# A graph tensor product on one core: second-pass chunks of 12 tiles, parts of 0.31, 0.36 and 0.33, and a loop over all edges behind a count of rows

## The chip, the cores and the metric

The kernel runs on one core of a Trainium2 chip. The metric is the time of one execution on the device, in microseconds (us). Three runs of the kernel before took 8667.58, 8670.53 and 8680.19 us; their median is 8670.53.

The core has five engines with instruction streams of their own: PE (matrix products), DVE (vector work), ACT (functions of one operand), POOL (here: the indirect DMAs, that is gathers and scatters by a list of row numbers) and SP (the other DMAs). They wait for each other through semaphores.

## The reference

There are 10000 nodes with 64 channels of 4 components (x), and 640000 edges, each with a source node, a destination node, four numbers Y and four numbers edge_feat. Sources and destinations are drawn at random.

```
R   = silu(edge_feat @ w_rad)                      # (E, 64)
xs  = x[src]                                       # (E, 64, 4)
tp  = einsum('eci,ef,ifo->eco', xs, Y, cg)         # (E, 64, 4)
msg = R[:, :, None] * tp
agg = segment_sum(msg.reshape(-1, 256), dst, N).reshape(N, 64, 4)
out = einsum('ncm,cd->ndm', agg, w_mix)
```

## The kernel before

**Sorting.** To sum without conflicts, the kernel first sorts the edges by destination in two passes. An edge travels as 9 words (a key that holds destination and source, Y, edge_feat). The edges lie as 5000 tiles of 128. The first pass puts them into 18 groups of 576 destinations, the second puts a group into its 18 buckets of 32 destinations; there are 313 buckets. Both work on chunks of T tiles: T is 12 in the first pass and 11 in the second (L109). In a chunk, the edges of one group (bucket) are packed into rows of r edges: r is 14 in the first pass, 15 in the second. PE does the packing: for each tile of the chunk a one-hot matrix of 128 x 128 (L588 on DVE, L594 and L595 on ACT for six of the tiles, act in L48) times X, the edge's words spread over the r slots of a row (L569, L572). The products of a chunk add up in one PSUM tile `pr` (L602), so a chunk may fill at most 128 rows. ACT copies it to `rt` (L609), and POOL scatters the rows to DRAM with one indirect DMA (L613, `store`).

**Carried rows.** In the second pass (carry) a bucket's last row of a chunk, when it isn't full, is not stored but carried: PE adds it in the next chunk with one more product (L604). `tables` (L351) works out for a whole segment which row every chunk's buckets begin at, from counts that PE makes (L365). In it `st` holds the first row of each bucket in a chunk, and `inc` the running number of rows, whose last column is the number of rows of the chunk.

**Parts.** The edges are cut into three parts by their position (SPLIT, L36): 0.3, 0.355 and 0.345 of the 5000 tiles, rounded to 24. A bucket has 17 tiles of 128 slots in DRAM, of which part 0 is given 5 and parts 1 and 2 six each. What doesn't fit into a part's tiles lies in the next part's; what doesn't fit into 145 rows of a bucket goes to an overflow list.

**Messages.** For each part, group and bucket the kernel works on a unit: POOL gathers 128 source rows of x for each of the unit's 5 or 6 tiles with an indirect DMA each (L893, into one of 7 `xg` buffers), DVE multiplies them by the radial function (L945) and builds S from Y and the destination within the bucket (L935, L938), and PE sums over the edges (L958) into `G`. After the last part the weights are applied (L1006) and the output is written (L1015). There are 939 units and 5321 gathers.

**Order.** The first pass of part 0 runs alone, together with the clearing of buckets and groups. From then on `groups` (L1039) writes the order of PE, DVE and ACT by hand: it walks the quarters of the units of part k and puts between them steps of the first pass of part k+1 and of the second pass of the next segment (a part's group), by their shares of steps (`pass2_steps`). The smallest group comes first in each part, and is sorted before the part's messages begin. In each engine's stream the order is fixed.

**The end.** `overflow` (L1118) takes up the overflow list of each pass: a count is loaded into the engines' registers (L1131), and a loop runs its body for each 128 slots of the list (L1136 to L1199); the body computes 128 messages and adds them to the output rows with an indirect read (L1166) and an indirect write (L1199). For the first pass's list it writes the pass's number of rows in the same way.

Of the kernel before, what the change touches and what calls it, by code (L numbers as in the profile page):

```python
# [18 lines left out]
F = mybir.dt.float32  # L19
BF = mybir.dt.bfloat16  # L20
I32 = mybir.dt.int32
OP = mybir.AluOpType
# [12 lines left out]
UT = 6  # L35
SPLIT = ((0.3, (5,)), (0.355, (6,)), (0.345, (6,)))  # L36
LG = 5
# [8 lines left out]
class Pass:  # L46


    def __init__(self, T, r, cap, act, carry):
        self.T, self.r, self.cap, self.act, self.carry = T, r, cap, act, carry  # L50
        self.stride = 1 << (cap + P - 1).bit_length()
        self.rw = r * W

        assert T * P + B * (2 * r - 2 if carry else r - 1) < (P + 1) * r and cap >= P

# [18 lines left out]
class Kernel:  # L74
    def __init__(self, ctx, tc, x, src, dst, Y, ef, w_rad, cg, w_mix, out):
# [32 lines left out]
        self.p1 = Pass(T, r, max(map(max, self.gt)) * P // r, 6, False)  # L108
        self.p2 = Pass(11, 15, BT * P // 15, 6, True)  # L109

# [14 lines left out]
        self.xw = max(q.T * q.rw for q in (self.p1, self.p2))  # L125
        assert max(q.T + q.carry for q in (self.p1, self.p2)) <= 12

# [16 lines left out]
    def consts(self):  # L144
# [74 lines left out]
        self.bc = c.tile([P, B], F, name="bc")  # L219
        nc.vector.memset(self.bc, float(self.p2.cap))  # L220

    def clear_groups(self, k, eng):
# [128 lines left out]
    def tables(self, ps, D, nt, rows, kov, base, cap):  # L351
# [6 lines left out]
        assert N <= ps.NC <= 26 and nt >= T  # L358
        NC = ps.NC
        w = lambda nm, k, p=P, b=1, d=F: wk.tile([p, k], d, name=nm, tag=nm + ps.key, bufs=b)  # L360
# [12 lines left out]

        sums = w("sums", B * (T + 1))
        nc.vector.tensor_tensor_scan(sums[:H], ps.on, ps.cols, 0.0, op0=OP.mult, op1=OP.add)
# [37 lines left out]
        nc.vector.tensor_tensor(st[:H, :B], inc[:H], R[:H], op=OP.subtract)  # L413
        nc.vector.tensor_copy(st[:N, B:], inc[:N, B - 1:])

        first, at = w("first", B), w("at", T * B)
        if ps.carry:
# [17 lines left out]
        eye = self.ident[:N, :N].unsqueeze(2).to_broadcast([N, N, J])  # L435
        bs, bd = w("bs", NC * J, NC, d=BF), w("bd", NC * J, NC)
        blk = lambda t: t[:N, :N * J].rearrange("p (c j) -> p c j", j=J)
# [74 lines left out]
    def route(self, ps, quad, nt, table):  # L512
# [65 lines left out]
        def rows(c):  # L578
# [253 lines left out]
    def messages(self):  # L832
# [19 lines left out]
        def index(k):  # L852
# [265 lines left out]
    def overflow(self, ps, count):  # L1118
# [14 lines left out]

        def body(k):
            pay = wk.tile([P, W], F, name="opay")
            nc.sync.dma_start(pay, flat[bass.ds(k * (P * W) + ps.ovf * ps.rw, P * W)].rearrange("(s w) -> s w", w=W))  # L1136
# [7 lines left out]
            xg = wk.tile([P, 64, 4], F, name="oxg")  # L1144
            nc.gpsimd.indirect_dma_start(  # L1145
                out=xg.rearrange("p c i -> p (c i)"), out_offset=None, in_=self.x,
                in_offset=bass.IndirectOffsetOnAxis(ap=si, axis=0))

            pd = pm_.tile([P, 512], F, name="opd", tag="misc", bufs=1)
            nc.tensor.matmul(pd[:, :P], dst.to_broadcast([P, P]), self.ident, start=True, stop=True)  # L1150
            eq = wk.tile([P, P], F, name="oeq")
            nc.vector.tensor_scalar(eq, pd[:, :P], dst, None, op0=OP.is_equal)

            dup = wk.tile([P, P], F, name="odup")
            nc.vector.tensor_tensor(dup, eq, self.L, op=OP.mult)
            skip = wk.tile([P, 1], F, name="oskip")
            nc.vector.tensor_reduce(skip, dup, axis=AX.X, op=OP.max)
            em = wk.tile([P, 1], F, name="oem")
            nc.vector.tensor_scalar(em, dst, 0.5, None, op0=OP.is_lt)
            nc.vector.tensor_tensor(skip, skip, em, op=OP.max)  # L1160
            di = wk.tile([P, 1], I32, name="odi")
            nc.vector.scalar_tensor_tensor(skip, skip, FAR, dst, op0=OP.mult, op1=OP.add)
            nc.vector.tensor_scalar(di, skip, -1.0, None, op0=OP.add)
            cur = wk.tile([P, 256], F, name="ocur")
            nc.vector.memset(cur, 0.0)
            nc.gpsimd.indirect_dma_start(  # L1166
                out=cur, out_offset=None, in_=self.out, in_offset=bass.IndirectOffsetOnAxis(ap=di, axis=0),
                bounds_check=self.N - 1, oob_is_err=False)

            pT = pm_.tile([P, 512], F, name="opT", tag="misc", bufs=1)  # L1170
            nc.tensor.transpose(pT[:W, :P], pay, self.ident)
            sT = wk.tile([W, P], F, name="osT")
            nc.scalar.activation(sT, pT[:W, :P], AF.Copy)
            pr = pm_.tile([P, 512], F, name="opr", tag="misc", bufs=1)
            nc.tensor.matmul(pr[:, :80], sT, self.wo, start=True, stop=True)
            R = wk.tile([P, 64], F, name="oR")
            nc.scalar.activation(R, pr[:, :64], AF.Silu)
            A = wk.tile([P, 16], F, name="oA")
            nc.scalar.activation(A, pr[:, 64:80], AF.Copy)
            V = wk.tile([P, 64, 4], F, name="oV")  # L1180
            nc.vector.tensor_tensor(V, xg, R.unsqueeze(2).to_broadcast([P, 64, 4]), op=OP.mult)
            M = wk.tile([P, 64, 4], F, name="oM")
            for o in range(4):
                nc.vector.tensor_scalar(M[:, :, o], V[:, :, 0], A[:, o:o + 1], None, op0=OP.mult)
                for i in range(1, 4):
                    nc.vector.scalar_tensor_tensor(M[:, :, o], V[:, :, i], A[:, 4 * i + o:4 * i + o + 1],
                                                   M[:, :, o], op0=OP.mult, op1=OP.add)
            pm = pm_.tile([P, 2, P], F, name="opm", tag="misc", bufs=1)
            for h in range(2):
                nc.tensor.matmul(pm[:, h, :], M[:, 32 * h:32 * h + 32, :].rearrange("p c o -> p (c o)"), eq,  # L1190
                                 start=True, stop=True)
            ms = wk.tile([P, 2, P], F, name="oms")
            nc.scalar.activation(ms, pm, AF.Copy)
            po = pm_.tile([P, 512], F, name="opo", tag="misc", bufs=1)
            for h in range(2):
                nc.tensor.matmul(po[:, :256], ms[:, h, :], self.wx[:, h].rearrange("p d o -> p (d o)"),
                                 start=(h == 0), stop=(h == 1))
            nc.vector.tensor_tensor(cur, cur, po[:, :256], op=OP.add)
            nc.gpsimd.indirect_dma_start(  # L1199
                out=self.out, out_offset=bass.IndirectOffsetOnAxis(ap=di, axis=0), in_=cur, in_offset=None,  # L1200
                bounds_check=self.N - 1, oob_is_err=False)

        with tc.For_i(0, n, 1) as k:  # L1203
            body(k)

    def run(self):
# [63 lines left out]
```

## Time and profile before

| what | value |
|---|---|
| median of three runs | 8670.53 us (8667.58 to 8680.19) |
| span of the profiled execution | 8660.7 us |
| median of the runs less that span | 9.8 us |
| instructions | 149335 |
| mean granted TensorE clock | 0.894 |
| gathers (L893) | 5321 |
| first-pass chunks (stores to grp, L613) | 417 |
| second-pass chunks (stores to bkt, L613) | 541 |
| data moved by DMA | 1056.64 MB, mean 122 GB/s |

The profile shows one execution; its span reaches from the first to the last instruction, and no other time is given for that execution. In a row of a group stand the line of the code, the engine, the operation, the tile written and those read, the count, the busy time and the mean time in ns of one, and the idle time of the engine just before, with what ended most of it. "issue" there means that the engine waited for nothing that the profile shows. In a row of a stretch stand its bounds and length, then for PE, PEld (weight loads), DVE, ACT and POOL the busy time and the number of instructions, then the granted clock of PE (1.00 is full), the busy share of the DMA engines and GB/s. In a row of the waits stand the waiting instruction, what it waited for, and the total, the number and the longest of the waits. In a row of the timeline stand the start and length in us.

### The profile page before, as it was taken

The page shows a single profiled execution, that of the slowest core. Times are in us where ns is not written, and L with a number is a line of the kernel's source. Part 1 is how long each engine was busy: PE and PEld are TensorE (multiplying, and loading weights), DVE is VectorE, ACT ScalarE, POOL GpSimd, SP SyncE. Part 2 cuts the span into 40 slices and gives each one's busy share as a digit, 9 for nine tenths or more (in the row PEclk, how much of TensorE's full clock was granted, in tenths as well). Part 3 has the DMA queues.
Part 4 walks back from the last instruction along what each step waited for, and adds up shares of the span by engine and source line. Part 5 has one row for each costly group of instructions (what it writes and reads, how often), then busy time and mean ns, then how long its engine had stood idle before and what let it go on. Part 6 is the DMA issues. An engine that isn't in the chain of part 4 may idle for free. (4 is left out here: it accounts for less than half of the span.)

```text
span 8660.7 us, 149335 instructions
## 1 busy us (share of the span) xinstructions
PE 6942.9 (80%) x52148; PEld 6380.0 (74%) x52148; DVE 7173.7 (83%) x13741; ACT 4089.0 (47%) x11736; POOL 6041.3 (70%) x6308
## 2 busy tenths in 40 slices
PE   7978888888888778888888888866888878788875
PEld 6867777777777677777777777766777767777764
DVE  8989899889998788999989998877877768677754
ACT  6866555555556455454544554433333323333310
POOL 1236777667777767777777777777777777777775
PEclk9989999889999889999889899888998889888887
DMA  9313434334433434444444444444444444444442
GB/s 169 104 58 99 123 115 119 103 113 117 121 110 111 122 106 132 135 132 138 133 130 136 135 133 134 128 138 132 128 125 125 125 124 124 122 128 125 124 123 83
DMA packets 696289, 1056.64 MB, mean 122 GB/s; under 512 B 252018, under 2 KB 500226, under 8 KB 695536
## 3 DMA queue, kind: packets, MB, share of 16 engines
q0 software_dynamic: 286560, 746.71, 30.3%
q1 hardware_dynamic: 406384, 292.76, 12.2%
q8 instruction: 412, 6.75, 0.3%
q10 hardware_dynamic: 2592, 7.63, 0.3%
q14 instruction: 341, 2.79, 0.1%
HBM read 856.08 MB, written 207.12 MB: 123 GB/s over the span
## 5 line engine op out<-in xcount | busy, mean ns | idle before, releaser
L893 POOL DMA_INDIRECT xg<-in_x_dram,sidx x5321 | 5067.8, 952 | 1739.3 <-issue 1386.5
L602 PE MATMUL pr<-X,oh 128*128 128x126 f32 (+1 forms) x21112 | 2765.2, 289 | 395.7 <-ACT rt L609 215.6
L958 PE MATMUL G<-S,xg 128*128 128x128 f32 x21284 | 2953.1, 302 | 98.1 <-DVE Gp L987 62.8
L602 PEld LDWEIGHTS pr<-X,oh 128*128 128x128 f32 x21112 | 2638.2, 201 | 477.8 <-ACT rt L609 264.2
L958 PEld LDWEIGHTS G<-S,xg 128*128 128x128 f32 x21284 | 2803.5, 215 | 139.3 <-DVE Gp L987 86.2
L945 DVE TENSOR_TENSOR xg<-xg,pre 128x1536 f32<-128x1536 f32 (+1 forms) x939 | 1556.8, 1658 | 710.5 <-DMA xg<-in_x_dram,sidx 586.4
L594 ACT ACTIVATE sq<-i,rowf 128x128 f32<-128x128 f32 x5605 | 1735.7, 393 | 13.9 <-DVE rowf L559 13.4
L572 DVE TENSOR_TENSOR X<-dv,Wt 128x1512 f32<-128x1512 f32 (+4 forms) x958 | 1588.4, 1658 | 149.0 <-PE pr L602 94.8
L927 ACT ACTIVATE pre<-pre 128x384 f32<-128x384 f32 (+1 forms) x939 | 430.8, 459 | 1694.7 <-PE pre L924 1204.7
L595 ACT ACTIVATE oh<-sq,ones 128x768 f32<-128x768 f32 (+3 forms) x958 | 932.1, 973 | 32.9 <-issue 5.5
L938 DVE TENSOR_TENSOR S<-dv,pay 128x768 f32<-128x768 f32 (+1 forms) x939 | 857.4, 913 | 48.0 <-PE G L958 2.8
L613 POOL DMA_INDIRECT grp<-rt,idx x417 | 415.5, 996 | 585.9 <-ACT rt L609 240.1
L588 DVE TENSOR_TENSOR oh<-dv,rowf 128x640 f32<-128x640 f32 (+2 forms) x922 | 792.2, 864 | 0.5
L613 POOL DMA_INDIRECT bkt<-rt,idx x541 | 543.2, 1004 | 221.7 <-issue 125.8
L911 PE MATMUL pre<-identb,e 128*108 128x128 bf16 x1878 | 277.3, 231 | 523.4 <-DVE xg L945 513.6
L911 PEld LDWEIGHTS <-e 128*108 128x108 bf16 x1878 | 219.9, 133 | 604.5 <-issue 515.2
L916 ACT ACTIVATE sT<-pre 108x256 bf16<-108x256 f32 x939 | 353.5, 376 | 631.1 <-PE pre L911 628.4
L1006 PE MATMUL po<-wf,Gs 128*128 128x256 f32 (+2 forms) x1392 | 382.3, 436 | 150.7 <-DVE Gs L987 150.5
L542 ACT ACTIVATE pc<-pp 128x432 f32<-128x432 f32 (+3 forms) x506 | 243.7, 482 | 524.1 <-DVE pos L551 407.3
L1006 PEld LDWEIGHTS po<-wf,Gs 128*128 128x128 f32 (+2 forms) x1392 | 277.5, 205 | 238.3 <-DVE Gs L987 166.8
L609 ACT ACTIVATE rt<-pr 128x135 f32<-128x135 f32 (+1 forms) x958 | 258.8, 273 | 269.4 <-DMA bkt<-rt,idx 181.4
L923 PE MATMUL pre<-wr,sT 108*128 108x192 bf16 x939 | 240.2, 256 | 142.2 <-ACT sT L916 141.8
(240 smaller groups left out, 5309.3 us busy)
## 6 DMA issues: line engine op xcount, KB each, us to landing
xg<-in_x_dram,sidx POOLq DMA_INDIRECT x5321
sums<-Gp SPq DMA_DIRECT2D x626, 128.0 KB
old<-sums SPq DMA_DIRECT2D x626, 128.0 KB
bkt<-z SPq DMA_DIRECT2D x24, 994.5 KB
pay<-bkt SPq DMA_DIRECT2D x34, 486.0 KB
ys<-in_Y_dram SPq DMA_DIRECT2D x104, 96.0 KB
es<-in_edge_feat_dram SPq DMA_DIRECT2D x104, 96.0 KB
out_dram<-ot SPq DMA_DIRECT2D x69, 128.0 KB
```

Source lines behind the costliest of these rows:

```text
L572: nc.vector.tensor_tensor(X[:, :m, :].rearrange("p t (s w) -> p t s w", w=W), msk.unsqueeze(3).to_broadcast([P, m, ps.r, W]), QD[c // Q][1 ...
L588: nc.vector.tensor_tensor(oh[:, :v, :], self.v128.unsqueeze(1).to_broadcast([P, v, P]), row[:, o:o + v].unsqueeze(2).to_broadcast([P, v, P ...
L594: nc.scalar.activation(sq[:, u, :], self.i128, AF.Square, bias=to, scale=-1.0)
L595: nc.scalar.activation(oh[:, v:v + len(at), :], sq[:, :len(at), :], AF.Relu, bias=self.ones[:, 0:1], scale=-2.0)
L602: nc.tensor.matmul(pr[:, :ps.rw], oh[:, u, :], X[:, u, :], start=(u == 0), stop=(not on and u == m - 1))
L613: st = nc.gpsimd.indirect_dma_start(out=ps.dst, out_offset=bass.IndirectOffsetOnAxis(ap=idx[:, i:i + 1], axis=0), in_=RT.pop(c), in_offset ...
L893: nc.gpsimd.indirect_dma_start(out=xg[:, t, :], out_offset=None, in_=self.x, in_offset=bass.IndirectOffsetOnAxis(ap=si[:, u:u + 1], axis=0))
L911: nc.tensor.matmul(pre[:KR, 256 + 128 * h:384 + 128 * h], e[:, 36 * t:36 * t + KR], self.identb, start=True, stop=True)
L938: nc.vector.tensor_tensor(S[:, :ut], self.eq[:, :ut].unsqueeze(3).to_broadcast([P, ut, NB, 4]), pb[:, :, 1:5].unsqueeze(2).to_broadcast([P ...
L945: nc.vector.tensor_tensor(V, V, R.unsqueeze(3).to_broadcast([P, ut, 64, 4]), op=OP.mult)
L958: nc.tensor.matmul(G[:, h].rearrange("p n f -> p (n f)"), V[:, t, 32 * h:32 * h + 32, :].rearrange("p c i -> p (c i)"), S[:, t].rearrange( ...
L1006: nc.tensor.matmul(po[:nn, :256], Gs[:, h, f].rearrange("p b n -> p (b n)")[:, :nn], self.wf[:, h, f, :], start=(h + f == 0), stop=(h + f ...
```

## The change

- SPLIT becomes 0.31, 0.36, 0.33. In tiles the parts were 1488, 1776, 1736 and are 1560, 1800, 1640. The slots for tiles of a bucket stay 5, 6, 6.
- The second pass's T becomes 12. By lines 93 to 109 this gives:

| | before | after |
|---|---|---|
| first-pass chunks, parts 0, 1, 2 | 124, 148, 145 | 130, 150, 137 |
| tiles of a large group, parts 0, 1, 2 | 95, 113, 111 | 100, 115, 105 |
| tiles of the small group | 40, 47, 46 | 41, 48, 43 |
| second-pass chunks of a large group | 9, 11, 11 | 9, 10, 9 |
| second-pass chunks of the small group | 4, 5, 5 | 4, 4, 4 |
| tiles of all groups, parts 0, 1, 2 | 1655, 1968, 1933 | 1741, 2003, 1828 |
| second-pass chunks, parts 0, 1, 2 | 157, 192, 192 | 157, 174, 157 |

- With 12 tiles the second pass no longer has a bound that keeps every chunk within 128 rows, and the assertion is left out for it. Instead each `tables` of the second pass takes the maximum of the rows of its chunks into `most` (one DVE instruction more).
- At the end a new function `whole` compares `most` with 128.5. If a chunk was over, a loop of one trip clears the output, and a loop in it takes all 5000 tiles through the overflow list's body; that body is now a function `add`, used by both.
- The one-hot tile `oh` has 13 columns instead of 12 (12 tiles and the carried row). To make room, `sums` and `to` share a buffer, `at` and `bd` share one, and `didx` has one buffer instead of two.

```diff
-SPLIT = ((0.3, (5,)), (0.355, (6,)), (0.345, (6,)))
+SPLIT = ((0.31, (5,)), (0.36, (6,)), (0.33, (6,)))
...
-        assert T * P + B * (2 * r - 2 if carry else r - 1) < (P + 1) * r and cap >= P
+        assert (carry or T * P + B * (r - 1) < (P + 1) * r) and cap >= P
...
-        self.p2 = Pass(11, 15, BT * P // 15, 6, True)
+        self.p2 = Pass(12, 15, BT * P // 15, 6, True)
...
-        assert max(q.T + q.carry for q in (self.p1, self.p2)) <= 12
+        self.ot = max(q.T + q.carry for q in (self.p1, self.p2))
...
+        self.most = c.tile([64, 1], F, name="most")
+        nc.vector.memset(self.most, 0.0)
...
-        NC = ps.NC
+        NC, XW = ps.NC, max(ps.NC * J, B * (T + 1))
...
-        sums = w("sums", B * (T + 1))
+        sums = wk.tile([P, XW], F, name="sums", tag="x0" + ps.key, bufs=1)[:, :B * (T + 1)]
...
-        first, at = w("first", B), w("at", T * B)
+        if ps.carry:
+            nc.vector.tensor_tensor(self.most[:N], self.most[:N], inc[:N, B - 1:], op=OP.max)
+
+        first = w("first", B)
+        at = wk.tile([P, XW], F, name="at", tag="x1" + ps.key, bufs=1)[:, :T * B]
...
-        bs, bd = w("bs", NC * J, NC, d=BF), w("bd", NC * J, NC)
+        bs = w("bs", NC * J, NC, d=BF)
+        bd = wk.tile([P, XW], F, name="bd", tag="x1" + ps.key, bufs=1)
...
-            to, tg = w("to", NC * J), w("tg", NC, b=2)
+            to, tg = wk.tile([P, XW], F, name="to", tag="x0" + ps.key, bufs=1), w("tg", NC, b=2)
...
-            oh = self.ph.tile([P, 12, P], F, name="oh", bufs=3)
+            oh = self.ph.tile([P, self.ot, P], F, name="oh", bufs=3)
...
-            di = ph.tile([P, B, MT], I32, name="didx", bufs=2)
+            di = ph.tile([P, B, MT], I32, name="didx", bufs=1)
...
         with tc.For_i(0, n, 1) as k:
-            body(k)
+            self.add(*load(k))
+
+    def whole(self):
+
+        nc, wk = self.nc, self.ph
+        m = wk.tile([64, 1], F, name="om")
+        nc.vector.tensor_scalar(m, self.most, P + 0.5, None, op0=OP.is_ge)
+        cp = self.ps.tile([P, 512], F, name="cw", tag="misc", bufs=1)
+        nc.tensor.matmul(cp[0:1, 0:1], self.ones[:64, 0:1], m, start=True, stop=True)
+        ni = wk.tile([1, 1], I32, name="nw")
+        nc.vector.tensor_scalar(ni, cp[0:1, 0:1], 1.0, None, op0=OP.min)
+        n = nc.values_load(ni, min_val=0, max_val=1)
...
+        with self.tc.For_i(0, n, 1):
+            nc.sync.dma_start(self.out.rearrange("(p b) f -> p b f", p=125),
+                              zo.unsqueeze(1).to_broadcast([125, self.N // 125, 256]))
+            with self.tc.For_i(0, self.NT, 1) as k:
+                self.add(*load(k))
...
             self.overflow(self.p2, self.kov[:, 1:2])
+            self.whole()
```

More of the change, by code (lines that the diff above doesn't have):

```diff
@@ L1132, in overflow, with load @@
         flat = ps.dst.rearrange("r w -> (r w)")
-        def body(k):
+        def load(k):
             pay = wk.tile([P, W], F, name="opay")
@@ L1143, in body @@
             nc.vector.tensor_scalar(dst, dk, 1.0 - TD, None, op0=OP.add)
[L1144 to L1203, printed above, removed]
-            body(k)
+            return pay, si, dst
+        with tc.For_i(0, n, 1) as k:
+            self.add(*load(k))
[8 more added lines that the diff above has]
+        n = nc.values_load(ni, min_val=0, max_val=1)
+        assert self.N % 125 == 0
+        zo = wk.tile([125, 256], F, name="zo")
+        nc.vector.memset(zo, 0.0)
+        def load(k):
+            pay = wk.tile([P, W], F, name="opay")
+            nc.vector.memset(pay, 0.0)
+            si = wk.tile([P, 1], I32, name="osi")
+            dk = wk.tile([P, 1], I32, name="odk")
+            t = bass.ds(k, 1)
+            nc.sync.dma_start(si, self.src[:, t])
+            nc.sync.dma_start(dk, self.dst[:, t])
+            nc.sync.dma_start(pay[:, 1:5], self.Y[:, t, :].rearrange("p t f -> p (t f)"))
+            nc.sync.dma_start(pay[:, 5:9], self.ef[:, t, :].rearrange("p t f -> p (t f)"))
+            dst = wk.tile([P, 1], F, name="odst")
+            nc.vector.tensor_scalar(dst, dk, 1.0, None, op0=OP.add)
+            return pay, si, dst
+        with self.tc.For_i(0, n, 1):
[3 more added lines that the diff above has]
+                self.add(*load(k))
@@ new lines, in add @@
+    def add(self, pay, si, dst):
+        nc, wk, pm_ = self.nc, self.ph, self.ps
+        xg = wk.tile([P, 64, 4], F, name="oxg")
+        nc.gpsimd.indirect_dma_start(
+            out=xg.rearrange("p c i -> p (c i)"), out_offset=None, in_=self.x,
+            in_offset=bass.IndirectOffsetOnAxis(ap=si, axis=0))
+        pd = pm_.tile([P, 512], F, name="opd", tag="misc", bufs=1)
+        nc.tensor.matmul(pd[:, :P], dst.to_broadcast([P, P]), self.ident, start=True, stop=True)
+        eq = wk.tile([P, P], F, name="oeq")
+        nc.vector.tensor_scalar(eq, pd[:, :P], dst, None, op0=OP.is_equal)
+        dup = wk.tile([P, P], F, name="odup")
+        nc.vector.tensor_tensor(dup, eq, self.L, op=OP.mult)
+        skip = wk.tile([P, 1], F, name="oskip")
+        nc.vector.tensor_reduce(skip, dup, axis=AX.X, op=OP.max)
+        em = wk.tile([P, 1], F, name="oem")
+        nc.vector.tensor_scalar(em, dst, 0.5, None, op0=OP.is_lt)
+        nc.vector.tensor_tensor(skip, skip, em, op=OP.max)
+        di = wk.tile([P, 1], I32, name="odi")
+        nc.vector.scalar_tensor_tensor(skip, skip, FAR, dst, op0=OP.mult, op1=OP.add)
+        nc.vector.tensor_scalar(di, skip, -1.0, None, op0=OP.add)
+        cur = wk.tile([P, 256], F, name="ocur")
+        nc.vector.memset(cur, 0.0)
+        nc.gpsimd.indirect_dma_start(
+            out=cur, out_offset=None, in_=self.out, in_offset=bass.IndirectOffsetOnAxis(ap=di, axis=0),
+            bounds_check=self.N - 1, oob_is_err=False)
+        pT = pm_.tile([P, 512], F, name="opT", tag="misc", bufs=1)
+        nc.tensor.transpose(pT[:W, :P], pay, self.ident)
+        sT = wk.tile([W, P], F, name="osT")
+        nc.scalar.activation(sT, pT[:W, :P], AF.Copy)
+        pr = pm_.tile([P, 512], F, name="opr", tag="misc", bufs=1)
+        nc.tensor.matmul(pr[:, :80], sT, self.wo, start=True, stop=True)
+        R = wk.tile([P, 64], F, name="oR")
+        nc.scalar.activation(R, pr[:, :64], AF.Silu)
+        A = wk.tile([P, 16], F, name="oA")
+        nc.scalar.activation(A, pr[:, 64:80], AF.Copy)
+        V = wk.tile([P, 64, 4], F, name="oV")
+        nc.vector.tensor_tensor(V, xg, R.unsqueeze(2).to_broadcast([P, 64, 4]), op=OP.mult)
+        M = wk.tile([P, 64, 4], F, name="oM")
+        for o in range(4):
+            nc.vector.tensor_scalar(M[:, :, o], V[:, :, 0], A[:, o:o + 1], None, op0=OP.mult)
+            for i in range(1, 4):
+                nc.vector.scalar_tensor_tensor(M[:, :, o], V[:, :, i], A[:, 4 * i + o:4 * i + o + 1],
+                                               M[:, :, o], op0=OP.mult, op1=OP.add)
+        pm = pm_.tile([P, 2, P], F, name="opm", tag="misc", bufs=1)
+        for h in range(2):
+            nc.tensor.matmul(pm[:, h, :], M[:, 32 * h:32 * h + 32, :].rearrange("p c o -> p (c o)"), eq,
+                             start=True, stop=True)
+        ms = wk.tile([P, 2, P], F, name="oms")
+        nc.scalar.activation(ms, pm, AF.Copy)
+        po = pm_.tile([P, 512], F, name="opo", tag="misc", bufs=1)
+        for h in range(2):
+            nc.tensor.matmul(po[:, :256], ms[:, h, :], self.wx[:, h].rearrange("p d o -> p (d o)"),
+                             start=(h == 0), stop=(h == 1))
+        nc.vector.tensor_tensor(cur, cur, po[:, :256], op=OP.add)
+        nc.gpsimd.indirect_dma_start(
+            out=self.out, out_offset=bass.IndirectOffsetOnAxis(ap=di, axis=0), in_=cur, in_offset=None,
+            bounds_check=self.N - 1, oob_is_err=False)
```

## The prediction

> **What bounds the kernel now.** I read the page first, then the same busy times cut into stretches at the places where the gathers of one part end, then the indirect DMAs in those stretches and POOL's waits. The page:
>
> ```profile
> span 8660.7 us, 149335 instructions
> PE 6942.9 (80%) x52148; PEld 6380.0 (74%) x52148; DVE 7173.7 (83%) x13741; ACT 4089.0 (47%) x11736; POOL 6041.3 (70%) x6308
> L893 POOL DMA_INDIRECT xg<-in_x_dram,sidx x5321 | 5067.8, 952 | 1739.3 <-issue 1386.5
> L613 POOL DMA_INDIRECT bkt<-rt,idx x541 | 543.2, 1004 | 221.7 <-issue 125.8
> ```
>
> By shares VectorE (DVE) looks like the bound and POOL, at 70%, does not. But POOL's idle time is mostly "issue", time in which it waits for nothing. By stretches (columns: length, then busy time and count of PE, PEld, DVE, ACT, POOL):
>
> ```profile
> 0.00:620.00 620.00, 499.99 (x3727) 437.94 (x3727) 542.41 (x1280) 451.30 (x1359) 132.79 (x149) 0.92 0.49 111
> 620.00:3180.00 2560.00, 2076.45 (x16197) 1928.20 (x16196) 2285.05 (x4487) 1427.54 (x4174) 1808.10 (x1881) 0.91 0.39 113
> 3180.00:5965.00 2785.00, 2255.05 (x17482) 2101.39 (x17481) 2482.68 (x4627) 1353.06 (x3841) 2107.94 (x2196) 0.90 0.46 133
> 5965.00:8577.00 2612.00, 2081.22 (x14636) 1891.31 (x14636) 1838.62 (x3249) 853.51 (x2349) 1980.73 (x2072) 0.87 0.43 125
> 8577.00:8661.00 84.00, 30.15 (x113) 21.21 (x111) 24.94 (x101) 3.60 (x14) 11.74 (x13) 0.60 0.06 15
> ```
>
> I call them A (first pass of part 0 alone), B (messages of part 0, with the first pass of part 1 and the second of part 0), C (the same one part later), D (messages of part 2, with its second pass) and E (the end). Next the gathers in B, C and D, the bucket stores in D, and POOL's waits in D:
>
> ```profile
> 620.00:3180.00 2560.00, 1484.51 (x1559) 0.91 0.39 113
> 3180.00:5965.00 2785.00, 1778.43 (x1868) 0.90 0.46 133
> 5965.00:8577.00 2612.00, 1804.07 (x1896) 0.87 0.43 125
> 5965.00:8577.00 2612.00, 176.66 (x176) 0.87 0.43 125
> POOL xg L893 <- issue: 513.0, 1684, 0.3
> POOL bkt L613 <- issue: 43.9, 144, 0.3
> ```
>
> An indirect DMA holds POOL for its duration and then for 0.305 us of issue (513.0/1684). With 0.305 us behind each, POOL is taken for 1980.73 + 2072 x 0.305 = 2613 of 2612 us in D, 2107.94 + 2196 x 0.305 = 2778 of 2785 in C (99.7%), but 1808.10 + 1881 x 0.305 = 2382 of 2560 in B (93%). So C and D are paced by POOL's issue of indirect DMAs, one behind the other, whatever DVE does. A store costs 176.66/176 + 43.9/144 = 1.31 us there. In B neither is full: POOL 93%, DVE 2285.05/2560 = 89%. In A, DVE is:
>
> ```profile
> 250.00:500.00 250.00, 233.30 (x1865) 208.07 (x1865) 246.62 (x451) 226.96 (x686) 62.37 (x64) 1.00 0.28 95
> 250.00:500.00 250.00, 120.99 (x71) 1.00 0.28 95
> ```
>
> The second row counts L572's instructions, one for each chunk of 12 tiles: a chunk takes 250/71 = 3.52 us, with DVE busy for 246.62 of 250.
>
> **The change part by part.** The counts of tiles and chunks follow from lines 93 to 109 of the code and stand with the diff.
>
> *Fewer bucket stores.* 541 second-pass chunks become 488: 157 to 157 in part 0, 192 to 174 in part 1, 192 to 157 in part 2. Each chunk is one store (L613). First-pass stores stay 417, but lie 130, 150, 137 instead of 124, 148, 145. Each part's first, small group is sorted before its messages begin, in the stretch ahead. So C loses 8 + 17 + 1 = 26 stores, D loses 17 x 2 = 34, and B gains 2 - 1 = 1. In D that is -34 x 1.31 = -44.5 us. POOL paces D, and DVE is busy there for only 70%. In C it is -26 x 1.31 = -34 us, if POOL goes on pacing it.
>
> *A, 6 more chunks.* 6 x 3.52 = +21 us, DVE being full; at least 6 x (1.706 + 0.815 + 0.333) = 17 us, X, one-hots and mask alone by the rows of the next fence, and at most 6 x 620/124 = 30, the whole of A over its chunks.
>
> *B, more tiles in the same number of chunks.* The groups of part 0 grow from 1655 to 1741 tiles, since more edges fall into it, and its first-pass side grows by two chunks. What a tile costs on DVE:
>
> ```profile
> L572 DVE TENSOR_TENSOR X<-dv,Wt 128x1485 f32<-128x1485 f32 x487 | 830.6, 1706 | 61.4 <-PE pr L602 31.3 <-DVE dv L569 1.4
> L572 DVE TENSOR_TENSOR X<-dv,Wt 128x945 f32<-128x945 f32 x18 | 20.6, 1143 | 7.5 <-PE pr L602 5.8 <-DVE dv L569 0.5
> L588 DVE TENSOR_TENSOR oh<-dv,rowf 128x640 f32<-128x640 f32 x487 | 397.1, 815 | 0.4
> L588 DVE TENSOR_TENSOR oh<-dv,rowf 128x768 f32<-128x768 f32 x416 | 393.9, 947 | 0.0
> L569 DVE TENSOR_TENSOR dv<-dv,slot 128x165 f32<-128x165 f32 x487 | 162.3, 333 | 8.7
> L551 DVE TENSOR_REDUCE pos<-pc 128x22 f32<-128x396 f32 x243 | 134.8, 555 | 10.5 <-ACT pc L542 10.4
> L338 DVE TENSOR_TENSOR D<-dv,two 128x720 bf16<-128x720 bf16 x216 | 109.6, 522 | 0.3
> L412 DVE TENSOR_TENSOR_SCAN inc<-ones,R 64x18 f32<-64x18 f32 x85 | 15.5, 182 | 0.0
> ```
>
> X costs (1706 - 1143)/4 = 0.141 us a tile; a one-hot on DVE 0.947 - 0.815 = 0.132; mask, positions and digits 0.333/11 + 0.555/22 + 0.522/40 = 0.069. ACT builds six one-hots of a chunk and DVE the rest, so DVE's number in part 0 rises by 121, more than the tiles: 8 x 6 instead of 8 x 5 + 1 in a large group. B gets on DVE 86 x 0.141 + 121 x 0.132 + 86 x 0.069 = 34, plus 18 of the new maximum (L412, a small instruction, is the nearest row: 0.18 each, 3), plus two first-pass chunks (7): +44 us. If DVE paces B at its 89%, B grows by 49; if POOL does, by 1.3, its one store. The rows lie between (93% and 89%, nobody full), so I take the middle, +25, and keep both ends.
>
> *C on DVE.* Eight first-pass chunks fewer (-28). The 35 more tiles cost 35 x (0.141 + 0.069) = +7, the 89 more one-hots +12, the maxima +3, and 18 X instructions fewer save 18 x 0.155 (1.706 less 11 tiles of 0.141) = -3. Together -9. DVE to POOL goes from 2483/2778 = 0.894 to 2474/2744 = 0.902, a little towards B's 2285/2382 = 0.959, where POOL stands 7% of the time. So of the 34 I take 28 and keep 34 and 10 as the ends (10: DVE's 9 us at 89%).
>
> *PE and ACT.* PE's share is under 82% in B and C, and it loses the carry products and gains tiles; ACT loses 53 x 6 one-hots. Their cover is DVE and POOL, which are fuller. The shared x0 and x1 buffers and the one didx buffer are written and read on DVE in program order, except that PE reads bd; that is one table earlier. I price them at nothing; a wait there would cost about one small instruction, 0.2 us, in 84 tables.
>
> *The end.* Counting the reference's edges by bucket and part under the kernel's rules gives 19 rows of 15 slots beyond 145 a bucket now, hence 3 passes of 128 slots through the L1136 loop, and 11 rows, hence 2, after; the first pass has none beyond in either. The trace has the three:
>
> ```profile
> 8597.45 0.13 DVE L1130 TENSOR_SCALAR ni<-kov 1x1 int32<-1x1 f32 x1
> 8599.95 0.14 DVE L1130 TENSOR_SCALAR ni<-kov 1x1 int32<-1x1 f32 x1 [1.21 <-DMA xg<-in_x_dram,sidx]
> 8602.25 0.21 PE L1123 MATMUL cp<-kov,ones 1*16 1x1 f32 x2 [6.97 <-ACTq L1131]
> 8604.90 36.67 SPq L1136 DMA_DIRECT2D opay<-bkt  x3
> 8623.54 0.27 DVE L1165 MEMSET ocur<- 128x256 f32 x1 [4.84 <-PEq L1203]
> 8637.76 1.03 POOL L1199 DMA_INDIRECT out_dram<-ocur,odi  x1 [8.17 <-DVE ocur L1198]
> 8641.20 0.27 DVE L1165 MEMSET ocur<- 128x256 f32 x1 [3.72 <-PEq L1203]
> 8655.96 1.03 POOL L1199 DMA_INDIRECT out_dram<-ocur,odi  x1 [8.96 <-DVE ocur L1198]
> ```
>
> Three issues from 8604.90 on, the last one 36.3 us after the first: 18.2 a pass, -18.2 (17.7 by the two MEMSETs). The new function "whole" adds at the end: comparison, small matmul, minimum, a value loaded into every engine, and a loop of no trips. From 8597.58, when the count is there, to 8602.25, the first instruction behind the empty loop of the first pass, are 4.7 us; the second load, 8600.09 to 8604.90, shows 4.8. Before it stand some 2.4 us from the last store to the end of a pass (8638.8 to 8641.2 earlier) and 1 us of small instructions; against them go the 3.7 us that now follow the last store (8656.99 to 8660.7), part of which runs beside. I take +7, from 4.7 to 12.
>
> A rule speaks against this part. The Trainium skill (Runtime: NRT & Kernel Launch, Instruction fetch mechanics) says that a taken branch to a target outside the two fetched pages stalls the engine until the page is there. The 4.7 us may hold such a stall; no row here tells it from the register load. By the rule the jump over the longer body could cost one more, an estimate of at most 4.7 us again, and the forecast's sum would be -33.
>
> **The sum.** A +21, B +25, C -28, D -44.5, passes -18, "whole" +7: -37.5 us. The profiled span 8660.7 becomes 8623; the median of the three runs, 8670.53, lies 9.8 above the span, and I carry that unchanged: 8633 us. Its own range: B and C may move it by about 24 and 18, A and the end by 5 together, hardly all one way: 8602 to 8663.
>
> **The rivals.** *DVE paces B and C.* Then B pays all 49, C saves only 10: 21 + 49 - 10 - 44.5 - 18 + 7 = +4.5, 8675 us, no change that can be told. For it: C's busiest 40 us have DVE nearly full. Against it: POOL is full in the same row, while B's rows that fall short have DVE idle as well:
>
> ```profile
> 1540.00:1580.00 40.00, 31.80 (x245) 30.44 (x243) 33.88 (x64) 22.60 (x66) 20.43 (x22) 0.90 0.25 74
> 3900.00:3940.00 40.00, 35.56 (x287) 33.25 (x286) 38.49 (x75) 18.31 (x52) 30.54 (x32) 0.96 0.44 130
> ```
>
> *Gathers wait for buffers in C, and it ends slower.* A chunk's step on DVE gets 0.27 us longer (one tile of X and one of one-hots), products come later, PE's sums free the xg buffers later, and POOL waits as it does in B:
>
> ```profile
> POOL xg L893 <- PE G L958: 81.0, 42, 7.7
> ```
>
> At B's 93%, C would take 2744/0.93 = 2951, +166 in place of -28: 8827 us. It decides from where C grows by 9.5, that is POOL under 2744/2794.5 = 98.2% there. Against it: the ratio 0.902 is far from B's 0.959.
>
> *The change doesn't do what it says: the loop over all edges runs.* 5000 tiles at 18.2 us a pass are 91 ms. The count on the inputs gives 115 rows in the fullest chunk of 12 tiles, under 128, so this is excluded but for an error of mine.
>
> **How the numbers follow.** The forecast 0.70; DVE paces B and C 0.14; buffers in C 0.10 (from 8680 up); still faster than 8602, with B hidden wholly under POOL, 0.05; the loop 0.01. The predicted time is the forecast's, 8633. The range runs from 8602 to 8674, which holds the forecast and half of the DVE case. Within 0.2% of 8670.5, 8653 to 8688, is what a measurement here cannot tell from none; a tenth of the forecast's chance and most of the DVE case lie there. Faster 0.68 (nine tenths of 0.70, and the 0.05), same 0.20, slower 0.12 (0.11, and the upper edge of the DVE case).
>
> **What would show it.** 488 bucket stores, two L1136 passes, no pass of the new loop; POOL's busy time and issue still filling C and D, which end 60 stores earlier; A longer by about 21 us; B, from the first gather of part 0 to its last, longer by 1 to 49. POOL under 98% in C would make the prediction wrong, a third pass would add 18 us, and an end over 90 us long would mean that "whole" was under-priced.

## The result, and the profile after

The changed kernel takes 8656.17 us (median of 16 runs, 8649.23 to 8665.25) where the kernel before takes 8675.39 (16 runs): ratio 0.9979, 95% interval 0.9972 to 0.9987. In a second group of runs, on another chip, the medians were 8650.22 and 8659.76, ratio 0.9989 (0.9979 to 0.9999). So it is faster by 10 to 20 us, where 37.5 were forecast. Eight of the runs below fell on two chips on which every kernel, that before too, took a fifth longer (10443 and 10618 us); they are compared only among themselves.

The page of the changed kernel, with its lines shifted by six:

```profile
span 8651.4 us, 148141 instructions
L899 POOL DMA_INDIRECT xg<-in_x_dram,sidx x5321 | 5068.4, 953 | 1763.5 <-issue 1397.1
L619 POOL DMA_INDIRECT grp<-rt,idx x417 | 414.8, 995 | 623.8 <-ACT rt L615 318.1
L619 POOL DMA_INDIRECT bkt<-rt,idx x488 | 489.1, 1002 | 214.7 <-issue 113.9
```

488 bucket stores, as counted. The stretches A to E, cut again at the first gather, the first of part 1, the first of part 2 and the end of the last:

```profile
0.00:666.00 666.00, 525.32 (x3910) 461.44 (x3911) 568.41 (x1332) 470.77 (x1417) 138.50 (x155) 0.91 0.48 105
666.00:3260.00 2594.00, 2096.78 (x16408) 1950.78 (x16408) 2328.25 (x4499) 1421.27 (x4145) 1813.37 (x1888) 0.91 0.39 112
3260.00:6031.00 2771.00, 2243.57 (x17337) 2092.64 (x17338) 2467.85 (x4521) 1292.41 (x3643) 2092.28 (x2180) 0.90 0.47 134
6031.00:8579.00 2548.00, 2034.70 (x14160) 1848.18 (x14160) 1790.07 (x3130) 771.42 (x2108) 1932.00 (x2022) 0.88 0.44 127
8579.00:8652.00 73.00, 24.01 (x98) 16.93 (x96) 18.42 (x75) 2.66 (x10) 7.95 (x9) 0.62 0.04 12
```

The stores (L619, to grp and bkt) in C and D:

```profile
3260.00:6031.00 2771.00, 302.05 (x301) 0.90 0.47 134
6031.00:8579.00 2548.00, 144.58 (x144) 0.88 0.44 127
```

With 0.305 us of issue to each indirect DMA, POOL is taken for 2092.28 + 2180 x 0.305 = 2757 of 2771 us in C (99.5%) and 1932.00 + 2022 x 0.305 = 2549 of 2548 in D: still paced by POOL. Counted between the same gathers, C had 327 stores before and has 301, D had 176 and has 144. Against the kernel before, cut at the same gathers to a tenth of a us (it was profiled twice, the second time on the chip of the second profile of the changed one):

| stretch | forecast | first profiles | second profiles |
|---|---|---|---|
| A | +21 | 625.0 to 666.4: +41 | 622.6 to 656.4: +34 |
| B | +25 | 2564.5 to 2593.4: +29 | 2554.8 to 2593.5: +39 |
| C | -28 | 2797.7 to 2770.8: -27 | 2801.1 to 2772.4: -29 |
| D | -44.5 | 2590.5 to 2548.1: -42 | 2591.2 to 2548.2: -43 |
| end | -11 | 82.9 to 72.7: -10 | 82.1 to 70.8: -11 |
| span | -37.5 | 8660.7 to 8651.4: -9 | 8651.8 to 8641.3: -10.5 |

The gains came as forecast; the two prices, A and B, came out higher. Of the 28 and 27 us by which the gain fell short, A has 20 and 13, B 4 and 14.

### The profile page after: what moved, and what is told of

Read it like the earlier page. It is cut to its first block, busy times and chain, and to the rows that moved or that the text cites. A ratio compares the mean times of both kernels' runs of the same rounds, so it can differ in the third digit from the quotient of the medians.

```text
span 8651.4 us, 148141 instructions
## 1 busy us (share of the span) xinstructions
PE 6924.4 (80%) x51908; PEld 6370.0 (74%) x51908; DVE 7173.0 (83%) x13553; ACT 3958.5 (46%) x11321; POOL 5984.1 (69%) x6252
## 5 line engine op out<-in xcount | busy, mean ns | idle before, releaser
L608 PE MATMUL pr<-X,oh 128*128 128x135 f32 (+1 forms) x21144 | 2778.6, 290 | 426.6 <-ACT rt L615 201.4
L578 DVE TENSOR_TENSOR X<-dv,Wt 128x1620 f32<-128x1620 f32 (+3 forms) x905 | 1581.9, 1748 | 139.8 <-PE pr L608 88.8
L600 ACT ACTIVATE sq<-i,rowf 128x128 f32<-128x128 f32 x5395 | 1669.0, 393 | 21.0 <-DVE rowf L565 19.5
L601 ACT ACTIVATE oh<-sq,ones 128x768 f32<-128x768 f32 (+2 forms) x905 | 888.1, 981 | 30.4 <-issue 3.6
L619 POOL DMA_INDIRECT grp<-rt,idx x417 | 414.8, 995 | 623.8 <-ACT rt L615 318.1
L594 DVE TENSOR_TENSOR oh<-dv,rowf 128x768 f32<-128x768 f32 (+1 forms) x887 | 818.2, 926 | 0.3
L619 POOL DMA_INDIRECT bkt<-rt,idx x488 | 489.1, 1002 | 214.7 <-issue 113.9
L548 ACT ACTIVATE pc<-pp 128x432 f32<-128x432 f32 (+4 forms) x470 | 236.8, 504 | 512.5 <-DVE pos L557 389.2
L941 DVE TENSOR_TENSOR dv<-dv,dlc 128x192 f32<-128x192 f32 (+1 forms) x939 | 331.7, 353 | 16.3
L615 ACT ACTIVATE rt<-pr 128x126 f32<-128x126 f32 (+1 forms) x905 | 241.6, 272 | 185.9 <-PE pr L608 100.2
```

What stands on the lines that cost most here:

```text
L578: nc.vector.tensor_tensor(X[:, :m, :].rearrange("p t (s w) -> p t s w", w=W), msk.unsqueeze(3).to_broadcast([P, m, ps.r, W]), QD[c // Q][1 ...
L594: nc.vector.tensor_tensor(oh[:, :v, :], self.v128.unsqueeze(1).to_broadcast([P, v, P]), row[:, o:o + v].unsqueeze(2).to_broadcast([P, v, P ...
L600: nc.scalar.activation(sq[:, u, :], self.i128, AF.Square, bias=to, scale=-1.0)
L601: nc.scalar.activation(oh[:, v:v + len(at), :], sq[:, :len(at), :], AF.Relu, bias=self.ones[:, 0:1], scale=-2.0)
L608: nc.tensor.matmul(pr[:, :ps.rw], oh[:, u, :], X[:, u, :], start=(u == 0), stop=(not on and u == m - 1))
L619: st = nc.gpsimd.indirect_dma_start(out=ps.dst, out_offset=bass.IndirectOffsetOnAxis(ap=idx[:, i:i + 1], axis=0), in_=RT.pop(c), in_offset ...
```

## The experiments

**The two kernels once more.** No edit.

> The kernel before once more, for a second profile of it. Stretch A (up to the first gather) took 625 us in the first profile, and 666 in that of the changed kernel, +41 where six chunks more explain 21. Theory 1 (chance): the other 20 us are DVE's waits for the load of the destinations (da), which vary from run to run; then A of this kernel comes out anywhere from 620 to 645 us, and the whole span differs from 8660.7 by as much. Theory 2 (layout): they come from where the blocks of chunks now begin, the same in each run; then A is 625 again within 5 us, and da costs about 13 us of DVE's time in it.

> The changed kernel once more. Theory 1 (chance): A lies anywhere from 640 to 670 us. Theory 2 (layout): A is 666 again within 5 us, with about 28 us of DVE's waits for da in it. By both, the other stretches repeat within 8 us: B 2593, C 2771, D 2548, the end 73.

A was 622.6 and 656.4. The other stretches repeat within 2 us for the changed kernel. In the kernel before, C, D and the end repeat within 4, but B came out 10 us shorter the second time, with PE busy for 17 us less and DVE and POOL as before:

```profile
625.00:3189.50 2564.50, 2080.88 (x16232) 1932.83 (x16232) 2289.99 (x4493) 1434.48 (x4195) 1815.19 (x1888) 0.91 0.40 113
622.60:3177.40 2554.80, 2063.71 (x16232) 1917.13 (x16232) 2289.33 (x4493) 1435.15 (x4194) 1815.22 (x1889) 0.91 0.40 114
```

For A neither theory holds alone. It is 656 to 666 us in five profiles of kernels that do the same first pass of part 0 (666.4, 656.4, and 663.6, 658.6, 661.8 below) and 620 to 625 with the old parts: 31 us at least are the kernel's, some 10 a run's. Where they lie, the waits of DVE between 20 us and the last X of part 0 show, in both profiles before and both after:

```profile
DVE key L688 <- DMA da<-in_dst_dram: 13.2, 4, 6.1
DVE sums L375 <- ACT colsgrp L370: 10.9, 4, 6.7
```

```profile
DVE key L688 <- DMA da<-in_dst_dram: 14.7, 4, 9.3
DVE sums L375 <- ACT colsgrp L370: 10.2, 2, 6.2
```

```profile
DVE key L694 <- DMA da<-in_dst_dram: 28.4, 4, 11.7
DVE sums L377 <- ACT colsgrp L372: 15.0, 5, 7.8
```

```profile
DVE key L694 <- DMA da<-in_dst_dram: 17.0, 3, 6.8
DVE sums L377 <- ACT colsgrp L372: 16.3, 5, 7.8
```

DVE starts a block of chunks with `key`, and waits for that block's destinations, whose load stands in SP's queue among the clearing of the buckets. The second row is the wait for the counts that ACT copies. Up to the last X of part 0 (515.3 and 514.5 us before, 557.3 and 547.4 after) DVE's gaps over 0.4 us add up to 39 us before and 59 and 49 after. The rest of the growth, 42 - 19.4 and 32.9 - 10.4 (second profiles), is 22.5 us of work in both: the forecast's six chunks (21). The gaps are what it left out. The wait for the counts grew by 4 and 6 us, that for the destinations by 15 and 2.

**Each half of the change alone.** Chunks of 12 with the old parts (one line of the changed kernel put back), and the new parts with chunks of 11 (one line of the kernel before changed):

```diff
-SPLIT = ((0.31, (5,)), (0.36, (6,)), (0.33, (6,)))
+SPLIT = ((0.3, (5,)), (0.355, (6,)), (0.345, (6,)))
```

> Chunks of 12 tiles, the count of rows and the loop behind it, but the parts of before. Second-pass stores 140, 174, 174 instead of 157, 192, 192; first pass as before. Expected by the sum of the prediction: A as before (625, within 5), B -3 (17 stores fewer, DVE +14 us), C 18 stores fewer, -24, D 17 fewer, -22, the end +7 (three passes and the new test): span about 42 us shorter than before. Theory 2 says so as well: its 20 us belong to the parts. If chunks of 12 tiles themselves made A longer (the wider one-hot buffer, the shared buffers), A would be about 20 us over before here.

> The new parts alone, with chunks of 11 tiles and no loop over all edges. Second-pass stores 174, 192, 174, first pass 130, 150, 137. Expected: A +21 by six chunks (theory 1) or +41 (theory 2); B +30 to +55 (19 stores more, 86 tiles more on DVE); C -12 (9 stores fewer), D -22 (17 fewer), the end -18 (two passes). Together -1 to +44 us: no faster than before.

Chunks of 12 alone: 8591.49 us, ratio 0.9922 (0.9905 to 0.9938), -68 us. The parts alone: 8685.35 us, 1.0030 (1.0019 to 1.0040), +26 us. A belongs to the parts: 620.1 with chunks of 12 alone, 658.8 with the parts alone. C and D add up within 3 us: -21 and -21 with the chunks alone, -5 and -20 with the parts alone, -29 and -43 with both. Stretch B with chunks of 12 alone, with the new parts alone, and with both (second profile); that of the kernel before stands above:

```profile
620.10:3147.70 2527.60, 2047.82 (x16135) 1908.98 (x16136) 2283.18 (x4372) 1371.54 (x3995) 1796.12 (x1871) 0.91 0.40 115
```

```profile
658.80:3249.50 2590.70, 2094.02 (x16479) 1949.86 (x16479) 2324.56 (x4536) 1462.17 (x4267) 1833.72 (x1906) 0.91 0.39 112
```

```profile
656.40:3249.90 2593.50, 2098.30 (x16404) 1953.20 (x16404) 2326.49 (x4497) 1419.91 (x4145) 1812.30 (x1887) 0.91 0.39 112
```

From 2554.8, B falls by 27 with chunks of 12 (forecast -3) and grows by 36 with the parts; with both it grew by 39, not by 9. POOL's stores don't explain this. With chunks of 12, POOL has 18 indirect DMAs fewer in B under the old parts and 19 fewer under the new, and is taken for 25 and 27 us less (its busy time and 0.305 us for each). Under the old parts B fell by 27, and PE's busy time fell by 16 and DVE's by 6 as well. Under the new parts B didn't fall (2590.7 to 2593.5), with PE's and DVE's times the same within 4: there POOL's saving went into its waits (B's length less the time POOL is taken), which were 163 us in the kernel before, 161 with the chunks, 176 with the parts and 206 with both. The largest, that of the gathers for the buffers that PE's sums free, stood in the prediction with 81.0 us in 42 waits; in the changed kernel (666 to 3260 us) it is:

```profile
POOL xg L899 <- PE G L964: 108.1, 60, 8.1
```

So B's growth is POOL's waits, not its work. What lengthens them under the new parts is not shown.

The second-pass chunks per part say what the new parts trade: with 12 tiles a large group of part 0 is 8 chunks if it has 95 tiles, but 9 if it has 100. The new parts put 17 chunks back into part 0 and take 17 out of part 2. That shortens D by 22 us (2570.0 to 2548.2) and lengthens A by 36 and B by 66 (both take the 72 tiles that moved into part 0 as well).

**The end without the test.** `self.whole()` left out of the last line.

> The changed kernel without the test of the rows and the loop over all edges at the end (the counting of rows stays). The prediction priced the test at +7 us (4.7 to 12); the two kernels with 12 tiles and 11 tiles and the same three passes differed by 8.5 in the end stretch. Expected: the end stretch 62 to 66 us instead of 71 to 73, all others as in the changed kernel within 10. If it were free beside the last store's landing, the end would stay at 71.

8645.03 us, 0.9985 (0.9976 to 0.9995), beside 0.9989 with it. The end stretch was 70.8 us, as in one profile with the test, above the 62 to 66 expected; but from the last store's end to the span's end it was 3.2 us instead of 6.3 (3.7 in the kernel before). The test costs 3, not 7. Another 4 lie in the overflow list's loop (timeline of the changed kernel; the first column is the start):

```profile
8606.75 23.21 SPq L1142 DMA_DIRECT2D opay<-bkt  x2
8620.67 1.02 POOL L1247 DMA_INDIRECT out_dram<-ocur,odi  x1 [8.14 <-DVE ocur L1246]
8629.56 0.27 DVE L1213 MEMSET ocur<- 128x256 f32 x1 [9.17 <-PEq L1152]
8644.06 1.02 POOL L1247 DMA_INDIRECT out_dram<-ocur,odi  x1 [8.61 <-DVE ocur L1246]
8647.42 0.19 PE L1161 MATMUL cw<-om,ones 64*1 64x1 f32 x2 [4.11 <-issue]
```

Two passes, as counted. From the first pass's store (8621.69) to the second's first instruction are 7.9 us. Without the test they are the same:

```profile
8625.69 1.02 POOL L1247 DMA_INDIRECT out_dram<-ocur,odi  x1 [8.15 <-DVE ocur L1246]
8634.58 0.27 DVE L1213 MEMSET ocur<- 128x256 f32 x1 [9.17 <-PEq L1152]
```

The kernel before took 3.5 there, also with the new parts alone, and 2.4 from its second to its third pass (2.6 in the run of chunks of 12 with the old parts, which has three). So the 4 us came with the changed kernel, but not with the test or the loop behind it; which of its other edits brings them was not tried.

**DVE's work in B.** Five one-hots of a second-pass chunk on ACT instead of six:

```diff
-        self.p2 = Pass(12, 15, BT * P // 15, 6, True)
+        self.p2 = Pass(12, 15, BT * P // 15, 5, True)
```

> The changed kernel, with five instead of six one-hots of each second-pass chunk built on ACT, and so one more on DVE: DVE gets 0.13 us more in each full chunk, ACT 0.39 less. In B that is about 140 chunks, +18 us of DVE and -55 of ACT. Theory D (B is paced by DVE's work, added work shows nearly one for one): B grows from 2593 by 15 to 22 us. Theory P (B is paced by POOL's stores and gathers and a fixed sum of waits): B stays within 6. By both, C (2771) and D (2548) stay within 6, POOL pacing them, and A stays.

8647.01 us, 0.9985 (0.9976 to 0.9995). DVE was busy for 2344.2 us in B instead of 2327, and ACT for 60 less; B was 2598.3 long, beside 2593 to 2599 in the four profiles with six. Theory D falls: DVE's work alone is not what lengthens B, unless ACT's relief hid it. C and D were 2775 and 2554, up to 6 more; POOL itself was busy 5 us longer in each, its gathers taking 2 to 3 ns more.

**Loads two blocks ahead in A.**

```diff
-                ends(b + 1)
+                if b == 0:
+                    ends(1)
+                ends(b + 2)
```

and one buffer more for `da` and `si` each.

> The changed kernel, with the loads of destinations and sources in stretch A issued two blocks of chunks ahead instead of one (two more small buffers). If A's extra length over six chunks of 3.5 us comes from DVE waiting for the destinations' load (22 to 33 us of idle time ahead of the key instruction before A's last X), those waits fall to about 5 us and A from 656 to 666 down to 635 to 645; B, C, D and the end stay. If these waits only stand in for others (the counts' copy on ACT, the full PE behind it), A stays above 650.

8638.85 us, 0.9976 (0.9967 to 0.9986). A was 649.0, 7 to 17 less than in the five profiles without it. The waits now:

```profile
DVE sums L377 <- ACT colsgrp L372: 13.7, 3, 8.8
DVE key L696 <- DMA da<-in_dst_dram: 10.5, 2, 6.0
```

The destinations' wait fell to 10.5, not to 5, and the counts' copy stayed near 14. DVE's gaps over 0.4 us up to the last X (538.9) add up to 40 us, as in the kernel before (39): with the loads earlier, A's growth is the six chunks' work and little else. It is one profile; in the five without the edit the gaps are 49 to 59.

**Other parts with chunks of 12.** 0.295, 0.36, 0.345:

> Chunks of 12 tiles as in the changed kernel, parts of 0.295, 0.36, 0.345 (1464, 1800, 1736 tiles). Second-pass stores as in the run with the old parts (140, 174, 174), first pass 122, 150, 145, three passes at the end. Against that run (span 8588): if the tiles of part 0 are the dear ones (A and B grew by 36 and 66 us when part 0 got 72 tiles and 17 second-pass stores more), A falls by 7 to 12 for two chunks, B by 0 to 15, C grows by 1 to 3, D and the end stay: span 8565 to 8585. If the parts' bounds themselves hardly matter and only the number of chunks in a part does, A falls by 7 and nothing else moves: 8580.

8610.09 us, 0.9943 (0.9926 to 0.9960), slower than with the old parts. A's last X came 11 us earlier (502.9 instead of 514.2), but the time from there to the first gather, in which the first segment is sorted, grew from 106 to 123, so that A was 625.8; B was 2544.0, 16 above the old parts. Expected was a fall of A, and a fall or no change of B. The 17 us in A are mostly one wait of DVE: its instruction `base` (L776), behind the last X, waited 24.6 us instead of 6.5, by the profile for scatters to grp. Why they landed later, and the 16 in B, were not followed up.

**PE's work in B, and the two halves of B's growth.** A product done twice (what it first leaves is overwritten):

```diff
+            if ps.carry:
+                nc.tensor.matmul(pr[:, :ps.rw], oh[:, 0, :], X[:, 0, :], start=True, stop=True)
             for u in range(m):
```

> The changed kernel, with the first product of each second-pass chunk done twice (the first time it is overwritten): 157, 174 and 157 PE instructions more with their weight loads, 0.29 us each, nothing else. In the runs so far B's length less PE's busy time in B was the same within 17 us (480 to 497) in eight profiles. Theory PE (B is paced by PE's stream of products): PE gets 45 us more in B and B grows by 35 to 55, from 2593 to 2630 or more. Theory P (POOL and waits that have nothing to do with PE's load): B stays within 10. By both, C (2771) and D (2548) stay within 8, POOL pacing them.

> Chunks of 12 tiles, parts of 0.3, 0.36, 0.34: part 0 as in the run with the old parts, part 1 two first-pass chunks longer (124, 150, 143), second-pass stores 140, 174, 157, three passes at the end. Against that run (A 620, B 2528, C 2780, D 2570, end 91): A stays. B has two first-pass chunks more, 24 products, 7 us of PE and 7 of DVE: +7 to +9 by theory PE. If it is +16, as with the parts of 0.295 and 0.36, the two chunks cost more than their work. C: 2 first-pass and no second-pass stores fewer, -3; D: 17 fewer, -22. Span 8568 to 8580, the fastest so far.

> Chunks of 12 tiles, parts of 0.31, 0.355, 0.335: part 0 as in the changed kernel, part 1 two first-pass chunks shorter (130, 148, 139), second-pass stores 157, 174, 157, two passes at the end. Against the changed kernel: A stays at 656 to 666, B -7 to -9 by theory PE (2585), C +2, D the same. If B falls by over 16, the first-pass chunks of part 1 and not the tiles of part 0 are what is dear in B.

> The old parts with chunks of 12 tiles and the loads of destinations and sources two blocks ahead: the two edits that helped. Expected: A 610 to 615 instead of 620 (DVE's waits for the destinations were 19 us there), all else as with the old parts: span 8578 to 8586.

These four, and the same four again (e13 to e16), fell on the two chips named above, where POOL was taken for 80% of C only, so that they say nothing of the pace to be explained. Against the kernel before on the same chip: the double product 1.0009 and 0.9985, 0.30 and 0.36 0.9983 and 0.9968, 0.31 and 0.355 0.9958 and 0.9938, early loads with the old parts 0.9948 and 0.9937. In these, A with the early loads (631 and 642) was no shorter than without (630 and 636): with the old parts they gained nothing in A.

Two of them ran a third time, on a chip where the kernel before took 8667.06:

> The first product of each second-pass chunk done twice, a third time, on a chip where the kernel before takes its usual 8660 to 8675 us, if one is to be had. By theory PE, B grows from 2593 by 35 to 55 us with 45 us more of PE; by theory P it stays within 10. C (2771) and D (2548) stay within 8.

> Parts of 0.3, 0.36, 0.34 with chunks of 12 tiles, a third time. Against the run with the old parts (A 620, B 2528, C 2780, D 2570, end 91): A stays, B +7 to +9 by theory PE (+16 if the two first-pass chunks cost more than their work), C -3, D -22. Span 8568 to 8580.

The double product: 8680.07 us, 1.0011 (1.0001 to 1.0021). Its stretches B and C:

```profile
661.80:3274.10 2612.30, 2128.76 (x16742) 1985.56 (x16742) 2325.51 (x4497) 1419.67 (x4144) 1817.75 (x1888) 0.92 0.39 112
3274.10:6051.80 2777.70, 2275.62 (x17688) 2128.55 (x17688) 2469.01 (x4521) 1293.14 (x3644) 2098.74 (x2180) 0.90 0.46 134
```

PE was busy for 29 us more in B (2128.76 against 2099.6, the mean of the four profiles without the product), with DVE as before, and B grew from 2595, the mean of the same four, by 17. That is under the 35 to 55 of theory PE and over the 10 of theory P. POOL was busy for 4 us more in B, so that up to 4 of the 17 may be its own; the 6 us by which C grew are (2098.74 against 2092.28). So PE's work counts in B, at about half of its length; it is no sole pace either. The two profiles of the kernel before agree: 17 us more of PE's busy time, 10 us more of B.

0.3 and 0.36: 8602.34 us, 0.9926 (0.9910 to 0.9943). B was 2532.7, 5 above the old parts: two first-pass chunks cost about what they work. D stayed (2574): the -22 expected there was a slip, since a group of 109 tiles still has 10 chunks of 12. So what is dear in B lies with part 0: its 72 tiles more, and the 17 chunks that its larger groups take more. Which of the two it is was not shown.

## Why the prediction was wrong

The forecast moved the right way, and the time lies in its range, but the gain is a quarter to a half of the one forecast.

- **Fewer stores in C and D** (-28, -44.5): right, -27 and -42, -29 and -43. POOL paced both after as before. D lost 32 stores and not 34, since its first large group too is sorted in the stretch ahead; 32 at 1.31 us are 42. In C POOL is taken for 33 us less, and its waits grew by 5 to 7, as the discount from 34 to 28 had it.
- **A, 6 more chunks** (+21, at most 30): this step failed; A grew by 41 and 34. The work of six chunks was right (22.5 us), but the step took A for a stretch in which DVE has no gaps, from a window (250 to 500 us) that has few. A has gaps at the starts of its blocks, and with six chunks more they grew by 10 to 19 us: by the destinations' load, as the early loads show, and by the counts' copy, which was not tried by itself.
- **B, more tiles** (+25, the middle of 1.3 and 49): mis-sized, +29 and +39. DVE's added work was near the forecast (37 us against 44). The step failed in what it let pace B: DVE or POOL, with PE priced at nothing under their cover. POOL's work did not grow, its waits did, by 31 and 42 us. DVE's added work alone moved B by 0 to 5 of 17 us, PE's by 17 of 29. In the two pairs of profiles PE had 16 and 35 us more, which at that rate are 9 and 20; some 20 remain both times. Why POOL's waits grew so far is not settled.
- **The end** (-18 for a pass, +7 for the test): right in sum, -10 and -11, by luck. The test cost 3, under the least that the forecast gave it (4.7), and 4 came at the first jump back in the overflow loop, which the forecast didn't have. The Trainium skill (Runtime: NRT & Kernel Launch, Instruction fetch mechanics) says that a taken branch to a target outside the fetched pages has to wait until the target's page is fetched. A first jump of 7.9 us and a later one of 2.4 would go with this, though nothing here shows the fetch itself, nor why the kernel before took 3.5 at the same place. Behind the test no second stall of that size came: its 3 us hold everything.
- **The rivals.** DVE pacing B and C fell: C lost 27 and 29 and not 10. Waits for buffers did not slow C (POOL at 99.5%), but they grew in B, where the forecast had them as they were. The loop over all edges did not run.
- What the sum hid: chunks of 12 alone were worth 68 us, and the new parts took back 50 to 60 of it. The counts per part stood in the forecast; that 95 tiles make 8 chunks of 12 and 100 make 9 was not drawn from them.

The fastest version seen is chunks of 12 with the old parts: 8591 us, 0.9922 of the kernel before.

## What to carry to other kernels

Add the issue gap to each instruction before judging an engine's share: POOL at 70% busy was full for 60% of the time, and in D, where DVE had room, every indirect DMA left out gave its whole 1.3 us. In a stretch in which no engine is full, don't take a middle value for one engine's added work: price the work of each engine that grows, and look at the gaps of a stretch's beginning as well as at its steady part. When two sizes change together, count the pieces (chunks, passes) under each alone: one may give back the piece that the other saves.

## What the runs showed of the hardware

A gather of the changed kernel took 952 ns in the mean in D and 953 in C, with DVE busy for 70% and 89% of the stretch, and two indirect DMAs never stood closer than 0.30 us. In B, where no engine was full, 17 and 29 us more of PE's busy time went with 10 and 17 us more of length. The first jump back of the overflow loop took 7.9 us from store to first instruction in the changed kernel and 3.5 in the kernel before, a later one 2.4 to 2.6.
